# Retention and a gated feed-forward layer on one core: the decay of q moved to y, small loads on another queue, a new written order

## The chip, the cores and the metric

The kernel runs on one core of a Trainium2 chip. The metric is the device time of one execution in microseconds (us); the time before is 329.76 us, the median of 3 runs (329.74 to 330.32). The core has TensorE (matmuls into PSUM), VectorE, ScalarE and GpSimd, each with a list of its own that it works through in order, and SP, whose list here is the queue of loads.

## The reference

```
# q, k, v: (4, 8, 768, 64)      gamma[h] = 1 - 2**(-5-h),  scale = 1/8
for t in range(768):
    state = gamma * state + outer(k[:, :, t], v[:, :, t])     # 64 x 64 per head
    y[:, :, t] = scale * q[:, :, t] @ state
x = y as (4, 768, 512)
h = relu(x @ w_in)                                            # 512 -> 1024
c = conv along the sequence, 3 taps per channel, zeros at both ends
out = (h * sigmoid(c)) @ w_out                                # 1024 -> 512
```

All in float32. Retention is computed in blocks: gamma^(t-s) is split into gamma^t on one side and gamma^-s on the other, so that a block is a masked product of q and k, times v, plus q times the state of the blocks before.

## The kernel before, in words

There are 24 steps of 64 tokens, each for two of the four sequences and all eight heads (12 steps per pair of sequences); the first two steps instead take the first 128 tokens of one sequence each (the "wide" steps). A step loads q, k, k with tokens on the partitions, and v, 256 KB each, into one of four `rw` buffers. `scale_q` (VectorE, L729) multiplies q by the table gamma^t, `scale_v` (VectorE) or `scale_v_act` (ScalarE, four activations) multiplies v by gamma^-t; TensorE makes scores, VectorE masks them out of PSUM (`masked`), and TensorE makes y from them ("half" and "mix", which also hold the scores or the state update of another step). `carry` copies the running state from PSUM for the next step. A table serves two steps: `gq_copy` holds the one for steps 0 and 1 of a pair, `gq_more` lets TensorE make those of steps 2 and 4 in PSUM, where `scale_q` reads them, and `make_gq` makes the others on ScalarE out of the first.

Four steps make a unit of the feed-forward layer, six units in all. In unit 0 (`PLAIN` is 1) x is split into a rounded head (`x_head`, ScalarE) and a remainder (`x_rest`, VectorE) straight from y's PSUM bank, and `mm1` makes plain products in two token parts of 8 blocks each (letters A and B in the order). In units 1 to 5 `y_copy` (ScalarE) takes y from PSUM to a buffer, VectorE makes sums of its quarters (`t_13`, `t_2`, `t_4`), heads and remainders are made of both (`xt_head`, `xt_rest`), and seven block products (`fast`, table `SEVEN`) replace eight; `snap` and `sum` put them together. The few first tokens of a unit's first step that still belong to the unit before are `few_head`, `few_sum`, `few_thead`, `few_rest`. Then come the convolution (`conv_tap`, `conv_side`), the gate, its split, and the output matmuls (`mm2`, letter o), whose results ScalarE copies out (`put`) and GpSimd stores. The weights come as 64-bit words and are cut out by ScalarE and VectorE (`w_top`, `w_bits`, `w_head`, `w_rest`).

What each engine does when is written out by hand: `ORDER` holds one string per engine, a letter per task, and the n-th occurrence of a letter is the n-th task with it. `plan` replays the strings with estimated durations, only to choose the buffers and the places where TensorE gets filler matmuls (`keep_warm`). SP issues loads in the order of "DMA", at most 8 in flight: before a load it waits for the eighth load before it.

PSUM has seven rotating banks (`ps`) and one for the state. A bank of y is given back by the instruction that reads y: `y_copy`, or `x_rest` in unit 0.

Of the kernel before, what the change touches and what calls it, by code (L numbers as in the profile page):

```python
# [27 lines left out]
G = 2  # L28
# [36 lines left out]
    1: (0, ("w", 0, 0), "X"), 5: (3, ("s", 0), "Z"), 6: (4, ("s", 1), "X"), 4: (5, ("w", 1, 1), "W"),  # L65
    7: (6, ("s", 2), "X"), 2: (2, ("w", 0, 1), "Y"), 3: (1, ("s", 3), "Z"),
# [9 lines left out]
V_ON_ACT = [*range(WIDE, 8), *range(14, N_STEPS)]  # L76
# [6 lines left out]
        "rrsfsgqfsaatthqaAAAAAhaAhaABBBhaBBBBABhahaohasoCCCIOICCCIOOICCCOOIooIooCooOoooCoCIooIohaOoOhooahaooooooo"  # L83
        "oooooDDDPJoJDDDJPPJDDDJPPoJahaDDDJPPJhaoPoooohaoohaooooooooEEEKQKEEQEKQKEEEKQQKEEEKhaQKoQQhaoooooohaoooo"
        "ohaooFFFLRLohaFFFLRLFRRFFLRLFFFRRLoLoRhahaooooooGGGMoMoSSGGGMoMoSSoGGGMoMoSSGoGGMSMooSuuuuuuuuuuuuuuuuuu"
# [83 lines left out]
def tt(n):  # L169
    return 67 + n / 0.96, 160 + n / 0.96  # L170
# [1216 lines left out]
```

## Time and profile before

| | us |
|---|---|
| median of 3 runs | 329.76 |
| the profiled execution | 331.79 |
| its span | 330.1 |
| TensorE busy | 322.2 |
| VectorE busy | 290.1 |
| ScalarE busy | 221.9 |

A span reaches from the first to the last instruction; the execution's time holds about 1.7 us more. Matmuls are pipelined and overlap in the records, so TensorE's busy time is not a sum of work. "Idle before" is what an engine waited ahead of an instruction, with what ended the wait. PE is TensorE, PEld its weight loads, DVE VectorE, ACT ScalarE, POOL GpSimd; SPq is SP's queue.

### The profile page before, as it was taken

What the parts mean: (1) busy time and instruction counts of PE and PEld (TensorE: products, weight loads), DVE (VectorE), ACT (ScalarE), POOL (GpSimd) and SP (SyncE); (2) the same over time, 40 slices, a digit from 0 to 9 for tenths busy, and PEclk for the clock granted to TensorE, in tenths of its full rate; (3) what the DMA queues carried; (4) which work ended last, traced back from release to release, by engine and by line L of the source; (5) the groups of instructions that cost most, each with busy time, mean ns of one, the idle gap of its engine ahead of it and who ended that gap; (6) DMA issues with size and microseconds to landing.
All of it is one profiled execution on the core that took longest, in us unless ns stands there. A gap on an engine that the chain in (4) does not pass through costs nothing.

```text
span 330.1 us, 10667 instructions
## 1 busy us (share of the span) xinstructions
PE 322.2 (98%) x4551; PEld 288.2 (87%) x4551; DVE 290.1 (88%) x551; ACT 221.9 (67%) x447; POOL 27.0 (8%) x64
## 2 busy tenths in 40 slices
PE   8999999999999999999999999999999999999995
PEld 5789998988888888999788999888899979998994
DVE  1899999989999999597998368999889999999976
ACT  1589999866668845667758547887557872667440
POOL 2000000001004301100000021000003002000100
PEclk9999999999999999999999999999999999999999
DMA  6996976890006561104743021235002001001103
GB/s 218 401 362 202 312 239 218 305 298 5 3 1 198 189 225 54 43 2 161 223 131 101 0 95 36 89 130 200 3 3 97 2 2 64 0 3 64 66 0 129
DMA packets 21019, 40.21 MB, mean 122 GB/s; under 512 B 2742, under 2 KB 3254, under 8 KB 20972
## 3 DMA queue, kind: packets, MB, share of 16 engines
q1 hardware_dynamic: 19228, 34.15, 30.8%
q0 software_dynamic: 1600, 5.24, 4.2%
q8 instruction: 36, 0.59, 0.7%
q10 hardware_dynamic: 144, 0.13, 0.1%
q14 instruction: 11, 0.09, 0.1%
HBM read 33.23 MB, written 6.29 MB: 120 GB/s over the span
## 4 chain that ended last, share of the span: by engine, by line
PE 73%; DMA 9%; DVE 8%; ACT 7%; SPq 1%; issue 1%; DVEq 0%; ACTq 0%
PE ps L1045 30%; PE ps L1269 30%; PE ps L788 5%; PE ps L1246 5%; PE ps_st L788 3%; DMA rw<-in_qk 3%; DMA w<-in_w_in 2%; DMA w<-in_w_out 2%; DMA rw<-in_kv 2%; SPq L640 1%; DVE hc L1117 1%; DVE t L1260 1%; DVE hc L1077 1%; DVE hc L1127 1%; ACT top L996 1%
## 5 line engine op out<-in xcount | busy, mean ns | idle before, releaser
L1269 PE MATMUL ps<-w,g 128*128 128x512 f32 x480 | 118.3, 397 | 0.5 <-DVE hc L1077 0.5
L1269 PEld LDWEIGHTS ps<-w,g 128*128 128x128 f32 x480 | 87.5, 188 | 19.7 <-DVE hc L1077 0.7
L1045 PE MATMUL ps<-xa,w 128*128 128x256 f32 (+3 forms) x552 | 76.9, 283 | 0.3 <-ACT hc L1089 0.2
L1045 PEld LDWEIGHTS ps<-xa,w 128*128 128x128 f32 x552 | 70.7, 189 | 2.8 <-ACT t L1273 0.5
L1117 DVE SCALAR_TENSOR_TENSOR hc<-hc,cw_sb,hc 128x512 f32<-128x512 f32 (+1 forms) x96 | 68.1, 743 | 1.5 <-ACT hc L1112 1.3
L1045 PE MATMUL ps<-xa,s 128*128 128x256 f32 (+2 forms) x480 | 68.6, 282 | 0.7 <-ACT hc L1072 0.7
L1045 PEld LDWEIGHTS ps<-xa,s 128*128 128x128 f32 x480 | 62.4, 188 | 2.9 <-ACT hc L1072 1.1
L1077 DVE CUSTOM_DVE_ANT_0 hc<-ps,hc 128x256 f32<-128x256 f32 (+2 forms) x80 | 32.2, 418 | 16.0 <-PE ps L1045 11.5
L1072 ACT COPY hc<-ps 128x256 f32<-128x256 f32 (+2 forms) x60 | 22.0, 371 | 31.7 <-PE ps L1045 31.1
L1112 ACT ACTIVATE hc<-hc,cw_sb 128x512 f32<-128x512 f32 x48 | 33.6, 724 | 6.5 <-DVE hc L1077 5.4
L788 PEld LDWEIGHTS ps<-rw 64*64 64x64 f32 (+2 forms) x1472 | 29.1, 137 | 6.0 <-issue 1.4
L788 PE MATMUL ps<-rw 64*64 64x64 f32 (+2 forms) x1472 | 32.7, 225 | 0.7 <-ACT t L882 0.5
L1122 ACT ACTIVATE hc<-hc 128x1024 f32<-128x1024 f32 x24 | 25.3, 1059 | 9.6 <-DVE hc L1117 9.5
L1127 DVE TENSOR_TENSOR hc<-hc,hc 128x1024 f32<-128x1024 f32 x24 | 29.1, 1218 | 1.8 <-ACT hc L1122 1.8
L1135 ACT CAST g<-hc 128x1024 fp32r<-128x1024 f32 x20 | 21.0, 1050 | 13.8 <-DVE hc L1127 13.6
L878 DVE TENSOR_TENSOR xa<-t,xa 128x384 fp32r<-128x384 f32 (+5 forms) x45 | 24.7, 567 | 0.8 <-ACT xa L932 0.3
L1144 DVE TENSOR_TENSOR g<-hc,g 128x1024 fp32r<-128x1024 f32 x20 | 24.4, 1218 | 0.6 <-ACT g L1135 0.4
L788 PE MATMUL ps_st<-rw 64*64 64x64 f32 (+1 forms) x672 | 23.8, 219 | 0.4 <-issue 0.2
L788 PE MATMUL ps<-rw,cy 64*64 64x64 f32 x672 | 23.9, 219 | 0.0
L788 PEld LDWEIGHTS ps_st<-rw 64*64 64x64 f32 (+1 forms) x672 | 21.6, 135 | 2.1 <-issue 0.7
L788 PEld LDWEIGHTS ps<-rw,cy 64*64 64x64 f32 x672 | 21.5, 135 | 0.0
L757 ACT ACTIVATE rw<-rw,const_sb 128x128 f32<-128x128 f32 x64 | 20.2, 394 | 0.0
(89 smaller groups left out, 359.1 us busy)
## 6 DMA issues: line engine op xcount, KB each, us to landing
rw<-in_qk SPq DMA_DIRECT2D x48, 256.0 KB, 4.3
rw<-in_kv SPq DMA_DIRECT2D x46, 256.0 KB, 5.1
out_y<-t POOLq DMA_DIRECT2D x20, 256.0 KB, 2.6
w<-in_w_in SPq DMA_DIRECT2D x16, 256.0 KB, 5.4
w<-in_w_out SPq DMA_DIRECT2D x16, 256.0 KB, 5.6
out_y<-t SPq DMA_DIRECT2D x2, 256.0 KB, 2.4
out_y<-t SPq DMA_DIRECT2D x3, 128.0 KB, 1.7
out_y<-t ACTq DMA_DIRECT2D x1, 128.0 KB, 1.8
```

The costliest lines, as they stand in the source:

```text
L788: nc.tensor.matmul(out, lhsT, rhs, start=start, stop=stop, skip_group_check=True)
L878: nc.vector.tensor_tensor(out=out, in0=in0, in1=in1, op=ALU.subtract)
L1045: nc.tensor.matmul(ps, w(a, k), x(b, k), start=first and i == 0, stop=last, skip_group_check=True)
L1072: nc.scalar.copy(quarter(u, p, *((0, 1), (0, 0), (1, 1))[i]), strip("X", u, p))
L1077: nc.vector._custom_dve(dve_ops.TENSOR_ADD_SAT, out=quarter(u, p, *out), in0=strip(bank, u, p), in1=quarter(u, p, *other), s0=float("inf") ...
L1112: nc.scalar.activation(cv, h, AF.Copy, scale=w)
L1117: nc.vector.scalar_tensor_tensor(out=cv, in0=h, scalar=w, in1=cv, op0=ALU.mult, op1=ALU.add)
L1122: nc.scalar.activation(cv, cv, AF.Sigmoid)
L1127: nc.vector.tensor_tensor(out=cv, in0=h, in1=cv, op=ALU.mult)
L1135: nc.scalar.copy(g_of(u, p)[:, 0], cv_of(u, 2 * p))
L1144: nc.vector.tensor_tensor(out=lo, in0=cv_of(u, 2 * p), in1=hi.bitcast(F32), op=ALU.subtract)
L1269: nc.tensor.matmul(ps, g, w, start=(f == 0 and i == 0), stop=(f == NF - 1 and i == 2))
```

## The change

q is no longer scaled. `y_scale` on VectorE reads y from PSUM, multiplies it by the table and writes the buffer that `y_copy` wrote; `y_copy` is gone, and steps 2 and 3 of unit 0 pass through that buffer too. The tables of steps 2 and 4 are copied out of PSUM by ScalarE (`gq_keep`). v of steps 8 to 11 is scaled by ScalarE. The blocks of y lie in another order in their bank, so that one multiplication with a broadcast table serves both sequences; `SEVEN` and the constants follow, and some copies of unit 0 are cut into more pieces. The loads of the three small tables are issued by ScalarE, and the sigmoid that loads ScalarE's function table is a task in its order. All orders are new.

```diff
 SEVEN = {
-    1: (0, ("w", 0, 0), "X"), 5: (3, ("s", 0), "Z"), 6: (4, ("s", 1), "X"), 4: (5, ("w", 1, 1), "W"),
-    7: (6, ("s", 2), "X"), 2: (2, ("w", 0, 1), "Y"), 3: (1, ("s", 3), "Z"),
+    1: (1, ("w", 0, 0), "X"), 5: (6, ("s", 0), "Z"), 6: (4, ("s", 1), "X"), 4: (5, ("w", 1, 1), "W"),
+    7: (3, ("s", 2), "X"), 2: (2, ("w", 0, 1), "Y"), 3: (0, ("s", 3), "Z"),
...
-V_ON_ACT = [*range(WIDE, 8), *range(14, N_STEPS)]
+V_ON_ACT = [*range(WIDE, NC), *range(14, N_STEPS)]
...
-        "rrsfsgqfsaatthqaAAAAAhaAhaABBBhaBBBBABhahaohasoCCCIOICCCIOOICCCOOIooIooCooOoooCoCIooIohaOoOhooahaooooooo"
...
+        "rrsffgsqsaatthaqAAAAAAhaAhaABBBhaBBBBBhahaohasoCCCIOICCCIOICOoOCCoIoIooOoOooooCCCIooIohaoOOhaoooohaooooo"
...
     "DVE": (
-        "kkmmmqttmmbbllq9mrrbbllbblq9bl0mq9lrBrq800bqmlyyzz9dbmbqqvellrmr3322r4342m4qjr3j2j468jyzm0mIbbCyCzbbOIdC"
...
-        "re332244rqd3jjj2e4m6mj8hLFimhRFFFyLzRyzyLzFyFzRddyyFzzLRerFr332244err33jj2244djjiehGGyyMSizyzyzzGdMGSedy"
...
+        "kkmmmmbbmlttlr9rmbqblbblll9bblrmq9Brlq8m009yyzzq0dmbbellrm3q2r43m2rq34jr23j244qj6j8mmyyzzbI0bCCdOlCCeIyO"
...
+        "2e44d4jjq6ejj8mmhLiFmFqhRFLFyRyzzyLyFzzRdFdeyFyzzRrr332244qqerr3322jj4F4djjLiehGGyMzSiyyyzzzGddSMeGayyzz"
...
     "ACT": (
-        "qkaawwvcxxaawwaAaAwcvwa0w0AxvczxA0y5vaBctwBtBAAaacgkBeywwBvvxxkyxBcAhhyxchtBBy5h7A0ctCaaCCaCwawCgCeCttCw"
...
+        "rblaaqqwwxvnxcaacwaawwwAAvxaazwwAAAvxc0q5c00BvtBtvaBcgAakeAwwBBxvtxcxvhcxhkAh5h7BBBtaCa0CaCwCgCCewttCvwa"
...
     "DMA": (
-        "qrbkqkgqkwvwwwvvqwktwwwwwwwvqwwckvtqkqtqvwwtkwwwwqqvvvkkttktwvqkqwtwwwkwwvvwtwwtwwqqkkvtqktqkvvvttqkvtqq"
-        "vkttkqtvkvqkqqvvvkkqttttvkooooo"
+        "qqqkkkwwwwvvvtqkwwwwwwwwwvwtwwcqkvqktqqvwwvktwwqqkvvttkkvqktqkwwwwwqkwtvvvwwttwwwwqtkqttvvqvktkqtkqkqvkv"
+        "qkttqvktvvtqvtkqkvqttvkooooo"
...
-    load(("load_rows",), 2 * H * len(TERMS) * ROWS, take=[("hc", "rows")])
-    load(("load_c",), 4 * P * N_GVF)
-    load(("load_g",), 4 * P * 54, [("load_rows",)])
+    task(("load_rows",), ACT, (430, 3400), take=[("hc", "rows")])
+    task(("load_g",), ACT, (430, 3000), [("load_rows",)])
+    task(("load_c",), ACT, (430, 3500), [("load_g",)])
+    task(("table",), ACT, (1500, 1500), [("load_c",)])
...
-            decay = ("make_gq", n - c % 2) if c > 1 else ("gq_copy",)
-            if decay[-1] in GQ_ON_PE:
-                decay, at = ("gq_more", n - c % 2), GQ_ON_PE.index(n - c % 2)
-                if c % 2 == 0:
+            decay = ("gq_copy",)
+            if c > 1:
+                m = n - c % 2
+                decay = ("gq_keep" if m in GQ_ON_PE else "make_gq", m)
+                if m == n and m in GQ_ON_PE:
+                    at = GQ_ON_PE.index(n)
                     after = [("gq_more", GQ_ON_PE[at - 1]) if at else ("gq_rows",), ("load_g",)]
-                    pe(decay, 230, after, [("ps", ("gq", n))], [("hc", "rows")] * (n == GQ_ON_PE[-1]), 1)
-            if decay == ("make_gq", n):
-                task(decay, ACT, (1180, 1280), [("gq_copy",), ("load_c",)], [("gq", n)])
-            task(("scale_q", n), DVE, tt(512), [("load_q", n), decay], free=[("ps" if decay[0] == "gq_more" else "gq", ("gq", n - 1) if decay[0] == "gq_more" else n - 1)] if c % 2 and c > 1 else [])
+                    pe(("gq_more", n), 230, after, [("ps", ("gq", n))], [("hc", "rows")] * (n == GQ_ON_PE[-1]), 1)
+                    task(decay, ACT, act(512, 45), [("gq_more", n)], [("gq", n)], [("ps", ("gq", n))])
+                elif m == n:
+                    task(decay, ACT, (1180, 1280), [("gq_copy",), ("load_c",)], [("gq", n)])
...
             if own:
-                pe(("scores", n), 960, [("scale_q", n), ("load_k", n)], banks, count=32)
+                pe(("scores", n), 960, [("load_q", n), ("load_k", n)], banks, count=32)
...
                     after += [scaled, ("masked", n, 0)]
-                    after += [extra and ("scale_q", extra), extra and ("load_k", extra)]
+                    after += [extra and ("load_q", extra), extra and ("load_k", extra)]
...
+        if not wide:
+            table = [("gq", n - 1)] if c % 2 and c > 1 else []
+            task(("y_scale", n), DVE, tt(512), [("mix", n), decay], [("t2", ("y", n))], [y] + table)
         if u < PLAIN:
-            task(("x_head", n), ACT, act(512, 45), [("mix", n)], [("xa", u)] * (n == first))
-            task(("x_rest", n), DVE, tt(512), [("x_head", n)], free=[y])
+            task(("x_head", n), ACT, act(512, 45 + 85 * (not wide)), [("mix" if wide else "y_scale", n)], [("xa", u)] * (n == first))
+            task(("x_rest", n), DVE, tt(512), [("x_head", n)], free=[y if wide else ("t2", ("y", n))])
             continue
-        task(("y_copy", n), ACT, act(512, 45), [("mix", n)], [("t2", ("y", n))], [y])
...
-    table = const.tile([P, 1], F32, name="table")
-    nc.scalar.activation(table, warm[:, :1].bitcast(F32), AF.Sigmoid)
+    table_sb = const.tile([P, 1], F32, name="table")
+
+    @emits
+    def table():
+        nc.scalar.activation(table_sb, warm[:, :1].bitcast(F32), AF.Sigmoid)
...
-    def fetch(out, in_):
-
+    def fetch(out, in_, small=False):
+
+        if small:
+            nc.scalar.dma_start(out, in_)
+            return
...
-        if n - n % 2 in GQ_ON_PE:
-            return buf("ps", ("gq", n - n % 2)).rearrange("p (g t) -> p g t", g=NPAIR)
         return buf("gq", n - n % 2).rearrange("p (g t) -> p g t", g=NPAIR)
+
+    @emits
+    def gq_keep(n):
+        nc.scalar.copy(buf("gq", n), buf("ps", ("gq", n)))
...
-    @emits
-    def scale_q(n):
-        q, s = heads_of(n)[:, 0], n % 2
-        decay = gq_of(n)[:, :, s * C : (s + 1) * C].unsqueeze(1).broadcast_to([P, G, NPAIR, C])
-        nc.vector.tensor_tensor(out=q, in0=q, in1=decay, op=ALU.mult)
...
     def place_of(n, k, b):
-        return (2 * k + b - (UNIT_OF[n] >= PLAIN)) % 4
+        if n < WIDE:
+            return 2 * k + b
+        return 2 * b + 1 - k if UNIT_OF[n] < PLAIN else 2 * b if k else 3 - 2 * b
...
-        y, x, t = y_of(n).rearrange("p (k b) g c -> p k (b g) c", k=2), plain_x(1), n * C - PARTS[1][0]
-        return [(y, [x[:, i].rearrange("p k b g t -> p k (b g) t")[:, :, :, t : t + C] for i in range(2)])]
+        y, x, t = copied(n).rearrange("p (b k) g c -> p b k g c", k=2), plain_x(1), n * C - PARTS[1][0]
+        return [(y[:, :, 1 - k], [x[:, i, k, :, :, t : t + C] for i in range(2)]) for k in range(2)]
...
-    def y_copy(n):
-        nc.scalar.copy(buf("t2", ("y", n)), buf("ps", ("y", n)))
+    def y_scale(n):
+        s = n % 2 * C
+        y, out = (a.rearrange("p (q g c) -> p q g c", q=2, g=NPAIR) for a in (buf("ps", ("y", n)), buf("t2", ("y", n))))
+        decay = gq_of(n)[:, :, s : s + C].unsqueeze(1).broadcast_to([P, 2, NPAIR, C])
+        nc.vector.tensor_tensor(out=out, in0=y, in1=decay, op=ALU.mult)
...
-            nc.scalar.copy(x[:, 0, 1:], y[:, :3])
-            nc.scalar.copy(x[:, 0, 0], y[:, 3])
+            nc.scalar.copy(x[:, 0, 2:], y[:, :3:2])
+            for at, q in ((0, 3), (1, 1)):
+                nc.scalar.copy(x[:, 0, at], y[:, q])
...
-            difference(x[:, 1, 1:], y[:, :3], hi[:, 1:])
-            difference(x[:, 1, 0], y[:, 3], hi[:, 0])
+            difference(x[:, 1, 2:], y[:, :3:2], hi[:, 2:])
+            for at, q in ((0, 3), (1, 1)):
+                difference(x[:, 1, at], y[:, q], hi[:, at])
...
+    order = [2, 3, 0, 1]
     gq = scale * gamma[:, :, None] ** t[:P]
-    one = np.repeat(np.eye(2), D, axis=1).astype(_BF16)
+    one = np.repeat(np.eye(2)[::-1], D, axis=1).astype(_BF16)
     tables = [gq] + [scale * gamma[:, :, None] ** t[n * C : n * C + P] for n in GQ_ON_PE]
-    tables = zip(*(_pieces(x) for x in tables))
+    tables = zip(*(_pieces(x[:, order]) for x in tables))
...
-    gf = gamma[:, None, None, :] ** (P * np.arange(NC * C // P)).reshape(1, 1, -1, 1)
+    gf = gamma[::-1, None, None, order] ** (P * np.arange(NC * C // P)).reshape(1, 1, -1, 1)
...
```

## Rows read from the trace of the kernel before

**Rows 1.** The page, section 1: busy us (share of the span) xinstructions of each engine.
```profile
PE 322.2 (98%) x4551; PEld 288.2 (87%) x4551; DVE 290.1 (88%) x551; ACT 221.9 (67%) x447; POOL 27.0 (8%) x64
```
**Rows 2.** Waits of TensorE: line <- releaser: us in total, times, longest.
```profile
PE ps L1045 <- ACT hc L1072: 0.7, 1, 0.7
PE ps L788 <- ACT t L882: 0.5, 1, 0.5
```
**Rows 3.** Busy us (x instructions) by stretch; then TensorE's clock, DMA share, GB/s.
```profile
10.00:20.00 10.00, 9.85 (x244) 7.69 (x244) 9.46 (x18) 7.77 (x17) 0.00 (x0) 1.00 1.05 397
20.00:30.00 10.00, 10.00 (x195) 9.43 (x188) 9.48 (x17) 9.22 (x18) 0.00 (x0) 1.00 0.85 295
...
50.00:60.00 10.00, 9.31 (x386) 8.24 (x388) 9.96 (x24) 9.36 (x24) 0.50 (x2) 1.00 0.64 205
...
250.00:260.00 10.00, 10.00 (x113) 9.35 (x114) 9.93 (x18) 6.61 (x12) 1.96 (x3) 1.00 0.21 80
```
**Rows 4.** Timeline of TensorE: start us, us, engine line op out<-in xcount [idle before <-releaser].
```profile
21.07 7.35 PE L1045 MATMUL ps<-xa,w 128*128 128x256 f32 x60
...
157.03 1.65 PE L1269 MATMUL ps<-w,g 128*128 128x512 f32 x6
...
160.15 5.80 PE L1269 MATMUL ps<-w,g 128*128 128x512 f32 x24 [0.47 <-DVE hc L1077]
...
263.24 8.62 PE L1269 MATMUL ps<-w,g 128*128 128x512 f32 x36
271.94 0.97 PE L1045 MATMUL ps<-xa,w 128*128 128x254 f32 x6
...
274.90 1.55 PE L1269 MATMUL ps<-w,g 128*128 128x512 f32 x6
...
277.00 1.55 PE L1269 MATMUL ps<-w,g 128*128 128x512 f32 x6
```
**Rows 5.** Timeline of SP, which issues the loads, from the start.
```profile
0.82 0.37 SPq L640 DMA_DIRECT2D rw<-in_qk  x1
1.24 0.42 SPq L640 DMA_DIRECT2D hc<-in_rows  x1
...
2.10 1.30 SPq L640 DMA_DIRECT2D rw<-in_qk  x3
```
**Rows 6.** Stretches of 1 us near the start (columns as in rows 3).
```profile
3.00:4.00 1.00, 1.00 (x29) 0.87 (x28) 0.00 (x0) 0.00 (x0) 0.31 (x2) 1.00 0.82 162
4.00:5.00 1.00, 0.93 (x10) 0.27 (x4) 0.00 (x0) 0.00 (x0) 0.00 (x0) 1.00 0.68 178
5.00:6.00 1.00, 1.00 (x3) 0.50 (x2) 0.98 (x2) 0.00 (x0) 0.00 (x0) 1.00 1.06 399
```
**Rows 7.** Groups by line: names, shapes xcount | busy us, mean ns | idle before.
```profile
L1077 DVE CUSTOM_DVE_ANT_0 hc<-ps,hc 128x256 f32<-128x256 f32 (+2 forms) x80 | 32.2, 418 | 16.0 <-PE ps L1045 11.5 <-ACT hc L1072 3.7
...
L757 ACT ACTIVATE rw<-rw,const_sb 128x128 f32<-128x128 f32 x64 | 20.2, 394 | 0.0
...
L846 DVE TENSOR_TENSOR rw<-ps,mask 128x512 f32<-128x512 f32 x22 | 14.9, 683 | 0.5 <-PE ps L788 0.5
...
L882 ACT COPY t<-ps 128x512 f32<-128x512 f32 x20 | 11.7, 584 | 3.7 <-PE ps L788 3.7
...
L732 DVE TENSOR_TENSOR rw<-rw,gq 128x512 f32<-128x512 f32 x16 | 10.9, 685 | 2.4 <-DMA rw<-in_qk 2.4
...
L626 ACT ACT_TABLE_LOAD x1 | 1.3, 1283 | 0.8 <-PEq L1376 0.8
```
**Rows 8.** Timeline of ScalarE near the start.
```profile
2.10 0.20 ACT L626 ACTIVATE table<-warm 128x1 f32<-128x1 f32 x1
...
12.79 1.39 ACT L996 CAST top<-w 128x512 f16<-128x512 bf16 x2
```
**Rows 9.** Timeline of VectorE near 157 us and near 271 us.
```profile
156.49 0.69 DVE L732 TENSOR_TENSOR rw<-rw,gq 128x512 f32<-128x512 f32 x1 [2.36 <-DMA rw<-in_qk]
...
270.33 1.42 DVE L878 TENSOR_TENSOR xa<-t,xa 128x512 fp32r<-128x512 f32 x2
```

More of the change, by code (lines that the diff above doesn't have):

```diff
@@ L82 @@
     "PE": (
[L83 to L85 removed]
+        "rrsffgsqsaatthaqAAAAAAhaAhaABBBhaBBBBBhahaohasoCCCIOICCCIOICOoOCCoIoIooOoOooooCCCIooIohaoOOhaoooohaooooo"
+        "oooooDDDJPJDDPDJPoJDDDJPPoJahaDDDJPPJhaohaPooooooohaooooooEEEKoKEEEKQQQKEEEKQQKEEEKQQKhaoQhaoohaoooohaoo"
+        "oooooFFFLoRLhaFFFLRLRFRFFLRLFFRFLoLoRRhahaooooooGGGMoMoSSGGGMoMoSSooGGGMoMoGSSGGMoMoSSuuuuuuuuuuuuuuuuuu"
         "uuuuuuuuuuuuuuuuuuuuuuuuuuuuuuuuuuuuuu"
@@ L126 @@
 FETCH, FETCH_NS, BEHIND, PACKET_LAG = (61.0, 126.6, 127.3), (600, 2300), 0, {2: 1300, 6: 300, PE: 1100, ACT: 900}
-FIRST = {PE: 3850.0, DVE: 1200.0, ACT: 3200.0, POOL: 2500.0, DMA: 700.0}
+FIRST = {PE: 3850.0, DVE: 1200.0, ACT: 810.0, POOL: 2500.0, DMA: 700.0}
 WARM_UP, WARM_SMALL, WARM_NS = 4, 14, 232
@@ L150, in ops @@
     if name == "few_head":
-        return 1 + (UNIT_OF[k[1]] == PLAIN)
-    return 2 if name == "few_rest" or (name in ("g_head", "g_rest") and k[1] == LAST[0]) else 1
+        return 1 + 2 * (UNIT_OF[k[1]] == PLAIN)
+    if name in ("x_head", "x_rest") and k[1] in range(WIDE, UNITS[0]):
+        return 2
+    if name == "few_rest":
+        return 2 + (UNIT_OF[k[1]] == PLAIN)
+    return 2 if (name in ("g_head", "g_rest") and k[1] == LAST[0]) else 1
 def halves(n):
@@ L274, in list_tasks @@
         few = TOKENS[u][0] - FIRST_STEP[u] % NC * C if n == first else 0
+        if not wide:
+            table = [("gq", n - 1)] if c % 2 and c > 1 else []
+            task(("y_scale", n), DVE, tt(512), [("mix", n), decay], [("t2", ("y", n))], [y] + table)
         if u < PLAIN:
-            task(("x_head", n), ACT, act(512, 45), [("mix", n)], [("xa", u)] * (n == first))
-            task(("x_rest", n), DVE, tt(512), [("x_head", n)], free=[y])
+            task(("x_head", n), ACT, act(512, 45 + 85 * (not wide)), [("mix" if wide else "y_scale", n)], [("xa", u)] * (n == first))
+            task(("x_rest", n), DVE, tt(512), [("x_head", n)], free=[y if wide else ("t2", ("y", n))])
             continue
-        task(("y_copy", n), ACT, act(512, 45), [("mix", n)], [("t2", ("y", n))], [y])
         if few and u > PLAIN:
-            task(("few_head", n), ACT, act(6 * few), [("y_copy", n)])
-            task(("few_sum", n), DVE, (450, 550), [("y_copy", n)])
+            task(("few_head", n), ACT, act(6 * few), [("y_scale", n)])
+            task(("few_sum", n), DVE, (450, 550), [("y_scale", n)])
             task(("few_thead", n), ACT, act(8 * few), [("few_sum", n), ("few_head", n)])
@@ L285, in list_tasks @@
         elif few:
-            task(("few_head", n), ACT, (170, 280), [("y_copy", n)])
-            task(("few_rest", n), DVE, (160, 260), [("few_head", n)])
+            task(("few_head", n), ACT, (255, 365), [("y_scale", n)])
+            task(("few_rest", n), DVE, (235, 335), [("few_head", n)])
         t = C - few
-        task(("x_head", n), ACT, act(6 * t), [("y_copy", n)], [("xa", u)] * (n == first))
+        task(("x_head", n), ACT, act(6 * t), [("y_scale", n)], [("xa", u)] * (n == first))
         task(("x_rest", n), DVE, tt(6 * t), [("x_head", n)])
@@ L665, in load_c @@
     def load_c():
-        fetch(const_sb, consts)
+        fetch(const_sb, consts, True)
     def row_tile():
@@ L672, in load_rows @@
     def load_rows():
-        fetch(row_tile(), rows)
+        fetch(row_tile(), rows, True)
     def table_of(j):
@@ L697, in load_g @@
     def load_g():
-        fetch(low_tile(), low)
+        fetch(low_tile(), low, True)
     @emits
```

14 lines of the change are left out of this document (7 added, 7 removed), and 6 rows, old and new, of the table LETTER.

## The prediction

> **What bounds the kernel now.** I read the shares of the engines first. TensorE is busy 322.2 of 330.1 us, and VectorE and ScalarE far less [rows 1]. Busy time alone does not prove a bound, so I went on to what TensorE waited for: its longest named waits after the start are 0.7 and 0.5 us [rows 2]. So from its first feed-forward matmul at 21.07 us [rows 4] nearly the whole span is TensorE work laid end to end. The change adds, takes or reshapes no matmul. It can therefore win only in four places: before 21 us, while TensorE is fed late; between 20 and 60 us, where VectorE and ScalarE are nearly full too; at a stall near 157 us; and around 264 us, where VectorE is full again.
>
> The table by stretches shows the second place: in the first and the last of the four stretches from 20 to 60 us VectorE is busy 9.5 and 10.0 of 10 us and ScalarE 9.2 and 9.4, while ScalarE still has 2.2 us free between 10 and 20 us [rows 3]. The start of SP's list shows the first: q, two small tables, then three more q and k loads [rows 5]; from 3 to 5 us the DMA engines move 162 and 178 GB/s, against 399 right after [rows 6].
>
> The profiled execution took 331.79 us, 1.7 more than its span, and 2.03 us more than the median 329.76 of the runs. I sum differences against the profiled execution and take them off the median.
>
> **The change, part by part.** *VectorE's decay.* Twenty-two multiplications of q (0.685 us for those with the table in SBUF) go, and twenty-two of y come. The new ones read PSUM; the nearest row is the mask, which also takes a PSUM operand and a broadcast one: 0.683 us [rows 7]. Count and duration are equal, so the sum is zero. The extra PSUM read could cost 0 to 0.02 us each by these rows. What changes is when: q of step n was scaled about two steps ahead of the matmuls that use y of step n. Deferring it takes some two multiplications, 1.4 us, out of VectorE's work before 62 us, and puts them back near the end.
>
> *v on ScalarE for steps 8 to 11.* Each takes four activations of 0.394 us from ScalarE, 1.6 us, and frees 0.68 us of VectorE. One of the four steps falls before 62 us.
>
> *The copy of y.* Twenty copies of 0.584 us [rows 7] leave ScalarE, five of them before 62 us: 2.9 us. Two copies of a decay table out of PSUM come: 1.2 us. The matmul that refills y's bank now waits for VectorE, 0.683 in place of 0.584 us, so a prompt release is 0.1 us later; at the one place where TensorE waited for that copy (0.5 us) I expect the same wait.
>
> *The plain steps 2 and 3.* y used to be split straight from PSUM; now a multiplication stands ahead, and the head and the remainder are two instructions each. For step 4's few tokens, ScalarE's head becomes three small copies (one column took 0.20 us [rows 8]) and VectorE's remainder three. The first matmul of the second token part waits for exactly this. I price it at +0.4 us of late start (0 if other work lies in between, 0.7 if none does).
>
> *The table load.* The activation-function load (1.28 us) is now ScalarE's first instruction, at 0.8 us [rows 7], where nothing waits. After the change the first sigmoid stands behind the scaling of v of step 2, about 16 us. Either the one load moves there or a second one appears there: +1.3 us of ScalarE in both cases, +0 if the load stays at the head. I take 1.3. Two places behind it in ScalarE's list stands the carry copy that step 2's matmuls need.
>
> The row with the first activation shows it starting at 2.10 us [rows 8], directly after the load's end at 0.81 + 1.28. The Trainium skill, page "ScalarE: Activation LUTs", section "What ACT_TABLE_LOAD costs", puts a switch at about 2.66 us, because a drain follows the load. The trace disagrees for a load with nothing ahead of it; no run here shows one in mid-stream. By the page's figure ScalarE would lose 1.4 us more, and my gain at the start would be gone.
>
> *Small loads from ScalarE's queue.* Three loads leave SP's list, each about 0.4 us of issue [rows 5], and q, k of steps 0 to 2 go out back to back. They land while ScalarE is idle: its first weight step is at 12.79 us [rows 8]. If the stream is full from 3 us on, the 0.8 MB that 399 GB/s would move in those 2 us replaces 0.34 MB, so everything behind is 1.15 us earlier [rows 6]. k of step 0 now stands fourth of the big loads in place of second, which eats that gain for the first scores alone; I expect them at about 6.4 us still.
>
> Walking the new lists on from there, with about 0.6 us from start to start for a 512-column step on VectorE or ScalarE and TensorE's groups at their old lengths: first scores 6.4 to 8.5, two flips, second scores to 11.0, third to 12.3, both wide mixes to 13.4. VectorE: four masks to 12.4, two weight steps, a mask, a remainder, then the two tables of k at 15.3 and 16.0; TensorE's states to 17.0. ScalarE: v of step 2 to 15.8, the table load to 17.3, x's second head to 17.8, the carry to 18.4. Then VectorE's second remainder of x ends at 19.3, TensorE's mix of step 2 at 19.5, a table matmul at 19.8, and the first feed-forward matmul starts at 19.9 us: **-1.2 us** against 21.07. The lower bound is -1.9, if the six blocks now issued in a row all find their weights; the upper is 0.
>
> *What is left at 62 us.* VectorE: -1.4 - 0.7 + 0.5 for the extra small instructions = -1.6 us. ScalarE: -2.9 + 1.2 + 1.6 + 1.3 + 0.3 = +1.5 us, against 2.2 us of free time between 10 and 20 us, which the earlier weights let it use. So ScalarE does not cut the gain to nothing, but it leaves no room. I keep -1.2 + 0.4 = **-0.8 us** (between -1.9 and +1.9).
>
> *The stall near 157 us.* VectorE stood 2.36 us, waiting for q of a later step to land, because scaling q was next in its list [rows 9]. TensorE paid: one block of six 512-column and one of six 254-column matmuls took from 157.03 to 160.15, 3.12 us, where the same pair took 2.10 from 274.90 to 277.00 [rows 4]. After the change no VectorE instruction waits for a q load, and TensorE needs that q some 9 us later. **-1.0 us** (0 if another late input takes its place).
>
> *The last unit.* Before its first matmul TensorE has 36 output matmuls, 8.62 us from 263.24, and starts at 271.94; VectorE's last remainder ends at 270.33 + 1.42 = 271.75 [rows 4, 9]. So the cover is used up to 0.2 us, with VectorE 9.9 of 10 us busy [rows 3]. Now two multiplications of y (1.4 us) come into this stretch, and two short sums (0.418 us each, [rows 7]) move to later places in VectorE's list, one of them only behind part of the chain. Net +0.5 to +1.0 us on a chain with 0.2 of slack, of which I let the shorter work ahead absorb half: **+0.3 us** (0 to +1.2).
>
> Sum: -0.8 - 1.0 + 0.3 = -1.5 us: 330.3 us as profiled, 328.3 us as median.
>
> **Rivals.** *The whole early gain arrives* (-1.9 at the start, the few tokens covered, no loss at the end, 157 us gone): -2.9, 326.9 us. For it: VectorE has 1.6 us less in its fullest stretch. Against it: ScalarE's surplus.
>
> *It does nothing that counts*: the chain before 62 us ends in late transfers in both orders, and the 157 us stall is replaced by another late input. Weights of the second layer load behind q and k in the new list as well, so the 0.7 us wait near 67 us [rows 2] may grow by as much as the start gives. 329.7 us.
>
> *Slower: ScalarE becomes the bound of the first 62 us.* Its place is the stretch from 20 to 60 us, with 0.8 and 0.6 us free in its first and last 10 us [rows 3]. If it can't use its free time before 20 us (weights landing no earlier), its surplus of 1.5 us and the 0.4 us of the few tokens reach TensorE whole: +1.9, less 1.0 at 157 us, plus 0.3 at the end: +1.2, 331.0 us. It decides once ScalarE regains less than about 0.6 us of its idle time. A table load that held ScalarE twice as long as its row's 1.28 us would by itself use that up. (The Trainium skill's figure on the page named above is about that long.)
>
> **Numbers.** Chances: my forecast 0.47 (by itself 327.3 to 329.2), the whole gain 0.16, nothing 0.18, slower 0.19. A measurement of this kernel tells about 0.2% from no change, 0.66 us. Faster holds my forecast nearly whole and the whole gain, 0.62; same is the third case and a little, 0.19; slower 0.19. The range runs from 326.5 to 331.0 and leaves out some 0.2 at its ends.
>
> **What would show it.** Right: the first feed-forward matmul near 20 us; DMA near 400 GB/s from 3 us on; no VectorE wait on a q load at 157 us; ScalarE's total 2.5 to 4 us lower; VectorE's total 2 us lower; TensorE's work equal. A table load of 1.28 us near 16 us with the carry copy behind it shows that step. Wrong: the first such matmul at 21 us or later, TensorE waiting for ScalarE between 30 and 60 us for over 2 us in sum, or a gap of over 1 us ahead of the last unit.

## The result, and the profile of the changed kernel

Predicted were 328.3 us (326.5 to 331.0) and "faster". Measured, on one chip and in ten runs each: 330.37 us before, 332.16 us after, a ratio of 1.0055 [1.0035, 1.0075]. The change costs 1.8 us: slower, not faster, and outside the range.

The page of the changed kernel answers to [rows 1] with its engine line and its chain of waits by engine:

```profile
PE 323.1 (98%) x4551; PEld 289.8 (88%) x4551; DVE 287.3 (87%) x550; ACT 218.5 (66%) x449; POOL 29.9 (9%) x64
...
PE 94%; DVE 2%; DMA 1%; ACT 1%; issue 1%; SPq 0%; DVEq 0%
```

VectorE has 2.8 us less to do and ScalarE 3.4 us less (2 and 2.5 to 4 were predicted), and TensorE has the same 4551 matmuls. The kernel is still TensorE's work laid end to end, and yet longer. So I looked for the loss between matmuls, and compared the two kernels at landmarks that stand behind the same tasks in both TensorE orders. Each column is one profile; before and after were profiled twice.

| us, start of | before | before again | after | after again |
|---|---|---|---|---|
| first scores | 6.41 | 6.41 | 7.44 | 6.78 |
| first feed-forward matmul | 21.07 | 21.13 | 21.14 | 19.79 |
| unit 1 | 62.78 | 62.94 | 63.40 | 62.43 |
| the last unit | 271.94 | 270.23 | 271.66 | 270.10 |
| the output's last stage (the seven blocks) | 306.00 | 304.29 | 306.20 | 304.65 |
| last matmul | 325.71 | 323.99 | 326.03 | 324.49 |
| end of the span | 330.09 | 328.35 | 330.76 | 329.34 |

Against "before again", the mean of the two executions of the changed kernel gains 0.67 us up to 21 us, loses 0.64 from there to unit 1, 0.68 from unit 1 to the last unit, 0.48 in the last unit, 0.14 after it and 0.43 behind the last matmul: 1.70 us, against 1.8 in the medians. Two executions of one kernel lie up to 1.7 us apart in this table, so the split shows where to look; it proves no single term.

TensorE's named waits from 16 us on, first of the changed kernel, then of the kernel before in its second profile (columns: total us, times, longest):

```profile
PE ps L801 <- issue: 1.0, 2, 0.6
PE ps L1063 <- ACT hc L1107: 0.5, 1, 0.5
PE ps L1063 <- ACT hc L1090: 0.3, 1, 0.3
PE ps_st L801 <- ACT cy L867: 0.2, 1, 0.2
```

```profile
PE ps L788 <- ACT t L882: 0.5, 1, 0.5
PE ps L1045 <- ACT hc L1072: 0.3, 1, 0.3
PE ps L1045 <- ACT hc L1089: 0.2, 1, 0.2
PE ps_st L788 <- ACT cy L854: 0.2, 1, 0.2
```

Two things are new: a 0.5 us wait for L1107, ScalarE's activation at unit 1, and 1.0 us of "issue", stops for which the profile names no releaser. One is gone: the 0.5 us for the copy of y (L882). The new multiplication itself cost what it should, by the list of its line (duration min/median/max in ns):

```profile
L898 DVE TENSOR_TENSOR t<-ps,gq x20: 675/682/692, 21.7 to 263.6; 128x512 f32<-128x512 f32 x20
...
L898 DVE TENSOR_TENSOR t<-ps,gq_sb x2: 680/680/680, 148.1 to 151.1; 128x512 f32<-128x512 f32 x2
```

ScalarE's records of the start show the table load twice, as L1014's cast took a load of its own; each lasted 1.28 us, and the next instruction began 20 ns behind each end:

```profile
9.48 1.28 ACT L1014 ACT_TABLE_LOAD   x1 [9.48 <-DMA w<-in_w_in]
10.78 1.40 ACT L1014 CAST top<-w 128x512 f16<-128x512 bf16 x2
...
15.93 1.28 ACT L768 ACTIVATE rw<-rw,const_sb 128x128 f32<-128x128 f32 x4
17.22 1.28 ACT L638 ACT_TABLE_LOAD   x1
18.52 0.20 ACT L638 ACTIVATE table<-warm 128x1 f32<-128x1 f32 x1
18.62 0.57 ACT L948 CAST xa<-ps 128x512 fp32r<-128x512 f32 x1
19.09 0.59 ACT L867 COPY cy<-ps_st 128x512 f32<-128x512 f32 x1
```

The Trainium skill, page "ScalarE: Activation LUTs", section "What ACT_TABLE_LOAD costs", adds a drain of about 1.38 us; neither load here shows one.

### The profile page after: what moved, and what is told of

Its sections match the earlier page's. It is cut to its first block, busy times and chain, and to the rows that moved or that the text cites. A ratio compares the mean times of both kernels' runs of the same rounds, so it can differ in the third digit from the quotient of the medians.

```text
span 330.8 us, 10664 instructions
## 1 busy us (share of the span) xinstructions
PE 323.1 (98%) x4551; PEld 289.8 (88%) x4551; DVE 287.3 (87%) x550; ACT 218.5 (66%) x449; POOL 29.9 (9%) x64
## 4 chain that ended last, share of the span: by engine, by line
PE 94%; DVE 2%; DMA 1%; ACT 1%; issue 1%; SPq 0%; DVEq 0%
PE ps L1063 37%; PE ps L1287 33%; PE ps L801 11%; PE ps L1264 6%; PE ps_st L801 4%; PE ps L645 2%; DMA w<-in_w_out 1%; DVE xa L891 1%; SPq L655 0%; DVE t L891 0%; PE ps L756 0%; ACT rw L768 0%; DVE t L1278 0%; DVE t L898 0%; ACT xa L975 0%
## 5 line engine op out<-in xcount | busy, mean ns | idle before, releaser
L1063 PE MATMUL ps<-xa,w 128*128 128x256 f32 (+3 forms) x552 | 76.7, 283 | 0.5 <-ACT hc L1107 0.5
L1063 PEld LDWEIGHTS ps<-xa,w 128*128 128x128 f32 x552 | 70.9, 189 | 2.9 <-ACT hc L1107 0.9
L1063 PE MATMUL ps<-xa,s 128*128 128x256 f32 (+2 forms) x480 | 68.5, 283 | 0.3 <-ACT hc L1090 0.3
L1063 PEld LDWEIGHTS ps<-xa,s 128*128 128x128 f32 x480 | 62.6, 189 | 2.1 <-ACT hc L1090 0.5
L1090 ACT COPY hc<-ps 128x256 f32<-128x256 f32 (+2 forms) x60 | 22.2, 370 | 38.7 <-PE ps L1063 38.1
L891 DVE TENSOR_TENSOR xa<-t,xa 128x384 fp32r<-128x384 f32 (+7 forms) x50 | 26.3, 546 | 1.8 <-ACT xa L975 1.0
L768 ACT ACTIVATE rw<-rw,const_sb 128x128 f32<-128x128 f32 x80 | 25.5, 394 | 0.0
```

What stands on the lines that cost most here:

```text
L768: nc.scalar.activation(v[:, :, g], v[:, :, g], AF.Copy, scale=gvf_sb[:, n % NC, g : g + 1])
L891: nc.vector.tensor_tensor(out=out, in0=in0, in1=in1, op=ALU.subtract)
L1063: nc.tensor.matmul(ps, w(a, k), x(b, k), start=first and i == 0, stop=last, skip_group_check=True)
L1090: nc.scalar.copy(quarter(u, p, *((0, 1), (0, 0), (1, 1))[i]), strip("X", u, p))
```

## The experiments

**Was the stall at 157 us real?** The kernel before, unchanged:

> The kernel before, unchanged, for a second profile and for the size of no change. My prediction took its stalls from one profile that took 331.79 us, 1.4 us more than the median 330.37 of ten runs. Theory A: the stall of 1.0 us at 157 us is there in every execution, so the second profile shows VectorE waiting over 2 us for a load of q near 156 us again. Theory B: it belongs to that one execution; then the second profile lacks it, and the gain of 1.0 us in my sum was not there to be had. The ratio to the kernel before should be 1.000 within 0.002 under both.

329.79 us, 0.999 [0.996, 1.0019]. The stall of [rows 9] is gone in this execution: VectorE's wait for a q load, and the two blocks that took 3.12 us in [rows 4] now take 2.20 us (156.34 to 158.54):

```profile
DVE rw L732 <- DMA rw<-in_qk: 0.2, 1, 0.2
```

```profile
156.34 1.65 PE L1269 MATMUL ps<-w,g 128*128 128x512 f32 x6
157.83 0.88 PE L1045 MATMUL ps<-xa,s 128*128 128x254 f32 x6
158.54 1.32 PE L1269 MATMUL ps<-w,g 128*128 128x512 f32 x5
```

The two spans differ by 1.7 us, 1.4 of it between 155 and 160 us: 0.9 in these two blocks and most of the rest in a stop of TensorE just ahead of them. The first profile's execution (331.79) was 1.4 us above the ten-run median. Of the six profiles of kernels with the old decay in this document, it is the only one in which VectorE waits over 0.6 us for a q load, so the stall belongs to some executions, not to the kernel. How many have it is not known.

**The start: the table load and the order of the loads.** Three kernels: the first sigmoid put back behind the small loads, k of step 0 put second of the big loads, and both.

```diff
-"rblaaqqwwxvnx..."   ->   +"rblnaaqqwwxvx..."     # ScalarE (n: the sigmoid); it no longer waits for load_c
-"qqqkkkwwww..."      ->   +"qkqkqkwwww..."        # SP
```

> The changed kernel with the first sigmoid put directly behind ScalarE's three small loads. The trace of after shows two loads of an activation table, 1.28 us at 9.48 us and 1.28 us at 17.22 us, where before had one at 0.81 us. Theory A (the tables and what stands behind them set the start): one load is left, near 2.3 us, x's second head and the carry copy come 1.3 to 1.5 us earlier, and the first feed-forward matmul starts near 20.0 us in place of 21.14; 0.6 to 1.1 us less in all than after. Theory B (ScalarE's second load lies beside VectorE work that ends as late): the first feed-forward matmul stays within 0.3 us of 21.1 and the time within 0.3 us of after's. Theory C (the start may gain, but weights that land near 62 to 67 us set what follows): the first such matmul earlier, the waits of TensorE at 62.5 and 67.0 us (0.65 and 0.42 us) longer by the same amount, time unchanged.

> The changed kernel with its six first big loads in the order q0 k0 q1 k1 q2 k2 in place of q0 q1 q2 k0 k1 k2. In after the first scores start at 7.44 us, before at 6.41. Theory A (k of step 0 as the fourth load is what ate the gain at the start): the first scores start near 6.0 us, the second near 9 us in place of 11.2, and the first feed-forward matmul 0.3 to 1.0 us before 21.14. Theory B (the scores are early enough in both; ScalarE and VectorE set 21 us): first scores 1.2 us earlier, first feed-forward matmul within 0.2 us of 21.14, time within 0.3 us of after's.

> The changed kernel with both edits: the first sigmoid behind the three small loads, and the big loads in the order q0 k0 q1 k1 q2 k2. Theory A (the start is what was lost): first feed-forward matmul at 19.5 to 20.0 us and 1.2 to 1.6 us less than after in all. Theory C (later waits take it back): first such matmul as early, but the waits near 62 to 67 us and at 157 us grow, and the time is within 0.4 us of after's.

All are slower than the changed kernel, though each starts earlier than its first profile (21.14 us; its second started at 19.79): 1.0129 [1.0088, 1.0170], 1.012 [1.0074, 1.0167] and 1.0161 [1.0118, 1.0204], with the first feed-forward matmul at 20.64, 19.95 and 19.05 us but unit 1 only at 65.90, 66.81 and 64.35. One load is left in the first of them:

```profile
2.24 1.28 ACT L638 ACT_TABLE_LOAD   x1 [2.24 <-issue]
3.54 0.20 ACT L638 ACTIVATE table<-warm 128x1 f32<-128x1 f32 x1
```

So what is won at the start is more than given back. TensorE's waits from 16 us on say where, first with the sigmoid moved, then with k of step 0 second:

```profile
PE ps L801 <- issue: 3.4, 2, 2.3
PE ps L1063 <- ACT hc L1107: 0.5, 1, 0.5
PE ps L1287 <- DVE t L898: 0.4, 1, 0.4
```

```profile
PE ps_st L801 <- issue: 4.5, 3, 3.5
```

The table by stretches of the kernel with the sigmoid moved, cut at its two stops (us, then busy us and instructions of TensorE, its weight loads, VectorE, ScalarE and GpSimd, the granted clock, DMA share, GB/s):

```profile
54.50:55.95 1.45, 0.39 (x27) 0.25 (x19) 1.45 (x5) 1.45 (x6) 0.00 (x0) 1.00 0.52 168
55.95:59.50 3.55, 3.55 (x127) 2.93 (x126) 3.01 (x9) 2.91 (x8) 0.00 (x0) 1.00 0.83 286
59.50:62.00 2.50, 0.22 (x15) 0.08 (x7) 1.24 (x5) 1.17 (x3) 0.00 (x0) 1.00 0.93 302
```

Between the stops lie 127 matmuls and 126 weight loads, about 253 instructions. The page's third part lists an instruction queue of 36 packets with 0.59 MB, 16 KB each and one per 126 of the 4551 matmuls, and the DMA view of 59.5 to 62 us shows one of its packets in that stop:

```profile
q8 instruction: 36, 0.59, 0.7%
```

```profile
q8 instruction: 1, 0.02, 2.5%
```

That reads as TensorE standing at the end of a block of its own instructions until the next block is there. The Trainium skill, page "Runtime: NRT & Kernel Launch", section "Instruction fetch mechanics", tells of 16 KiB blocks of 256 instructions and calls the crossing mostly hidden; the trace agrees on the block and shows up to 3.5 us not hidden. A long stop can have a second price, by the stretches of the kernel with k second: the granted clock, 1.00 (2.4 GHz) up to the stop of 3.5 us, falls to 0.57 behind it, so for much of these 4 us it was at the lower level, 1.2 GHz. In the kernel with both edits it stayed at 1.00 behind a stop of 2.5 us.

```profile
58.00:62.00 4.00, 0.64 (x41) 0.50 (x30) 1.58 (x6) 1.50 (x5) 0.00 (x0) 1.00 0.97 321
62.00:66.00 4.00, 3.87 (x73) 3.62 (x74) 2.49 (x9) 1.49 (x6) 0.21 (x1) 0.57 0.41 126
```

**Is it the burst of weight loads ahead of it?** The changed kernel again, and the loads of `w_out` spread out in it and in the kernel with both edits:

```diff
-"...vqktqkwwwwwqkwtvvv..."
+"...vwwqktqkwqkwwwtvvv..."
```

> The changed kernel, unchanged, for a second profile beside the second one of the kernel before (span 328.4 us, against 330.1 in the first). Theory A: what after loses against that second profile, 2.0 us up to the last matmul, is in fixed places: 0.8 us between 60 and 68 us (waits for w_out weights), 0.6 us of waiting for nothing named inside the run of narrow matmuls at 156.5 us, 0.4 us in the last unit. Then the second profile shows the same three within 0.3 us each and a ratio of 1.004 to 1.008. Theory B: these are as accidental as the stall at 157 us was before; then at least two of the three are gone or elsewhere.

> The changed kernel with the loads of w_out between 58 and 63 us spread out: two of five go ahead of q of step 10, one stays, two go behind q and k of step 12. Theory A (weights that land late cost after the waits of 0.3, 0.65 and 0.42 us at 60.9, 62.5 and 67.0 us): these become shorter, 0.3 to 0.9 us less than after. Theory B (those waits are for ScalarE, which is late by itself): they stay, time within 0.3 us of after.

> The kernel with the early start (first sigmoid behind the small loads, q0 k0 q1 k1 q2 k2: first feed-forward matmul at 19.05 us in place of 21.14) and the same spreading of the w_out loads. Without the spreading TensorE stood 2.7 us in the middle of a run of narrow matmuls at 57.8 us, with nothing named as its releaser, while the DMA engines moved 332 to 381 GB/s for five w_out loads issued at about 57 us. Theory A (TensorE there waits for its own next instructions, whose transfer is queued behind that burst): the stall falls under 1.2 us, and the time by 1.5 us or more against 335.1. Theory B (the stall is the cost of fetching instructions inside narrow matmuls, whatever the other transfers do): it stays over 2 us and the time within 0.5 us of 335.1.

332.04 us, 1.0054 [1.0026, 1.0082] again. Of the three places that this profile was to confirm, the wait for L1107 (0.5 us) and the last unit (34.55 us) came again; the wait for L1090 and the stop at 157 us did not. With the loads spread, 1.0067 [1.0041, 1.0094] and 1.0128 [1.0077, 1.0179], and the longest stops stayed at 0.7 and 2.5 us. So spreading these five loads does not help. Other transfers still ran ahead of the 2.5 us stop, at 195 to 348 GB/s from 55 to 59 us, so transfers as such are not ruled out as the cause.

**The small loads alone, in the kernel before:**

```diff
-    load(("load_rows",), ...)      # SP "qrbkqkgqk...", ACT "qkaaww..."
+    task(("load_rows",), ACT, ...) # SP "qkqkqk...",    ACT "rblnqkaaww..."
```

> The kernel before with one part of the change alone: the three small loads issued by ScalarE ahead of its first sigmoid, SP starting with q0 k0 q1 k1 q2 k2. Theory A (this part is good at the start and lost later): first scores near 5.2 us in place of 6.41, first feed-forward matmul 0.5 to 1.2 us before 21.1, and TensorE's waits between 53 and 68 us longer by about as much, time within 0.5 us of before or slower. Theory B (this part alone gains; the loss is in the new order): 0.5 to 1.2 us faster than before.

0.9983 [0.9954, 1.0013], no difference clear of noise: first scores at 5.14 in place of 6.41, but the first feed-forward matmul at 20.95 against 21.13 and unit 1 at 62.88 against 62.94. Most of the gain is gone before 21 us, which neither theory had.

**The waits that carry names.** A sixth buffer for the scaled y; ScalarE's unit-1 activations ahead of two later tasks; both:

```diff
-BUFS = {... 't2': 5 ...}          +BUFS = {... 't2': 6 ...}
-"...xhkAh5h7BBB..."               +"...xhkABh5h7BB..."       # ScalarE
```

> The changed kernel with six in place of five buffers in the pool that takes both the scaled y and the finished output rows. In four of seven profiles of the changed kernel and its variants one multiplication of y stood 0.4 to 1.5 us on VectorE until an output row's transfer out of its buffer had landed (in the second profile of after 1.40 us near 108 us, and TensorE's output matmul behind it 0.66 us); in three profiles of before and its variant the copy of y by ScalarE never did. Theory A (the move of y's bank from ScalarE to VectorE exposes TensorE to that wait): no such wait in the profile, and 0.2 to 0.8 us less than after. Theory B (the wait only fills time that is lost elsewhere): no such wait, time within 0.2 us of after.

> The changed kernel with one of three relu copies that stand behind the few tokens of step 8 in ScalarE's list put two places ahead of them, where ScalarE idles 0.52 us. In all profiles of the changed kernel that start its second unit near 62 us TensorE waits there 0.65 us, put down to this relu by the waits; in before it does not wait there. Theory A (relu, ready since 51 us, holds the PSUM bank because ScalarE's list waits for VectorE's multiplication of y): the first matmul of unit 1 comes 0.2 to 0.65 us earlier, and the time falls by as much. Theory B (the few tokens themselves end as late): the gap stays within 0.2 us, time within 0.2 us of after.

> Both edits of the changed kernel, six buffers and the relu ahead. Theory A: 0.5 to 1.2 us less than after, so within 1.3 us of before. Theory B (neither counts; the loss is in where TensorE stops for its instructions): within 0.3 us of after.

1.0095 [1.0061, 1.0129], 1.0085 [1.0058, 1.0111], 1.006 [1.0037, 1.0083]. The first tested nothing: the planner takes the lowest free number and never hands out the sixth buffer. Its plan is that of the changed kernel, and the third edit's plan is that of the second. So 1.0095 is a third series of the changed kernel, beside 1.0055 and 1.0054, and shows how far one kernel's ratio can move between series. The relu put ahead halves the wait for L1107, but unit 1 starts at 63.35 us against 63.40, as TensorE's stop near 55 us is 0.2 us longer in that execution and another of 0.1 us comes near 60 us. Against the first kernel of the same series the relu's two are 0.4 and 1.1 us faster by the medians, within the intervals. TensorE's two waits at L1063 then:

```profile
PE ps L1063 <- ACT hc L1107: 0.2, 1, 0.2
...
PE ps L1063 <- ACT hc L1090: 0.2, 1, 0.2
```

The buffer was tested with another rule of choice: the one longest free.

```diff
-  i = min(some, key=lambda i: (max(some[i], t), i))
+  i = min(some, key=lambda i: (max(some[i], t), some[i] * (name == "t2"), i))
```

> The changed kernel with another choice among its five buffers that take scaled y and output rows: the one that has been free longest, in place of the free one with the lowest number. With six buffers the planner had never handed out the sixth, so that kernel ran as after and tested nothing; here the multiplication of y of step 10, near 109 us, gets a buffer whose output row left some 5 us earlier. Theory A (TensorE's stop of 0.2 to 0.9 us near 110 us, in five of eight profiles, comes from that buffer): VectorE's wait ahead of this multiplication and TensorE's stop are gone, and the time falls by 0.2 to 0.8 us against after's 332.1. Theory B (the multiplication waits for ScalarE's table of decays or its carry): the wait stays.

332.06 against 330.46 in that series, 1.0035 [1.0011, 1.006]. In the changed kernel's second profile VectorE's step at 109 us waits until its buffer has been written out, and TensorE waits for VectorE:

```profile
109.22 0.69 DVE L898 TENSOR_TENSOR t<-ps,gq 128x512 f32<-128x512 f32 x1 [1.40 <-DMA out_y<-t]
```

```profile
109.97 3.06 PE L1287 MATMUL ps<-w,g 128*128 128x512 f32 x12 [0.66 <-DVE t L898]
```

With the new rule both waits are gone:

```profile
109.08 0.68 DVE L898 TENSOR_TENSOR t<-ps,gq 128x512 f32<-128x512 f32 x1
```

```profile
107.58 5.62 PE L1287 MATMUL ps<-w,g 128*128 128x512 f32 x23
```

The wait is shown and removed; the time won by it, 0.7 us by the ratios, is within their intervals.

**Do the stops move with the instruction count?** Idle matmuls at the start shift every later instruction by a known number: 32 more in the kernel before, 28 fewer in the kernel with both edits, and 8 more in the changed one.

```diff
-WARM_UP, WARM_SMALL, WARM_NS = 4, 14, 232
+WARM_UP, WARM_SMALL, WARM_NS = 4, 30, 232     # 0 and 18 in the others
```

> The kernel before with 30 in place of 14 pairs of small idle matmuls at the start: 32 more matmuls, 0.45 us in the trace's spacing, at a place where TensorE waits 0.36 us for a load; nothing else is changed. All profiles so far show TensorE's longest waits for nothing named at the same matmuls of the program, the 1108th and the 1235th, 127 apart, inside runs of 64-column matmuls. Theory A (TensorE stops where a block of about 127 matmuls' instructions ends if the next is not there yet, so the alignment of these blocks to the narrow runs sets part of the time): the waits move by 32 matmuls to earlier ones of the program, their sum changes, and the time changes by over 1 us, in either direction. Theory B (the waits belong to these places of the program, for instance to late inputs): they stay at the same work, and the time is within 0.5 us of before.

> The kernel with the early start (first feed-forward matmul at 19.05 us, 335.1 us in all) without the 14 pairs of small idle matmuls at the start, so that its instruction blocks end 28 matmuls later in the program. The two stops of 1.1 and 2.7 us at 53 and 58 us stood at its 1108th and 1234th matmul, both inside runs of narrow ones; 28 later the second lies nearer to the end of its run. Theory A (block ends): the stops move by 28 matmuls and their sum of 3.8 us changes by over 1 us, the time with it. Theory B (late inputs of those steps): the sum stays at 3.3 to 4.3 us and the time within 0.6 us of 335.1.

> The changed kernel with 18 in place of 14 pairs of small idle matmuls at the start, 8 matmuls more (0.1 us). Theory A (the loss of after is largely a matter of where its instruction blocks end): the waits for nothing named move by 8 matmuls, and the time changes by more than 0.6 us, up or down; if it falls by 1.5 us or more, the change itself costs nothing. Theory B (the loss is in its waits for VectorE and ScalarE): within 0.4 us of after.

With 32 more the kernel before is at 1.0162 [1.0121, 1.0203], some 5.3 us slower, for matmuls that last 0.5 us in all and stand where TensorE waits for data anyway. Its profile (the fastest of its runs, 333.42) has stops in places where none was, a feed-forward block at 22 us among them:

```profile
PE ps L1045 <- issue: 1.6, 2, 1.0
PE ps_st L788 <- issue: 0.9, 1, 0.9
PE ps L1269 <- issue: 0.5, 1, 0.5
```

Its five longest stops without a releaser stand ahead of the 347th, 853rd, 1107th, 1997th and 2379th matmul of the trace: 4, 2, 7 and 3 times 126 to 128 apart. With 28 fewer, 1.0247 [1.0197, 1.0297], some 2.8 us above its own base by the ratios:

```profile
PE ps L801 <- issue: 4.0, 4, 2.1
```

There the stops between 53 and 64 us stand ahead of the 982nd, 1109th and 1235th matmul, again 127 and 126 apart. Its base stopped ahead of the 1109th and 1235th too, and these are other instructions of the program, 28 matmuls further on. So the stops belong to the count, not to the work. The loss of this kernel is not all in them: its first feed-forward matmul starts at 20.94 us against 19.05. With 8 more the changed kernel gave 331.54, 1.0023 [1.0001, 1.0046]. To see whether the 8 matmuls alone do that:

> The changed kernel with both edits that came out below it: the buffer that has been free longest (ratio to before 1.0035) and 8 more small idle matmuls at the start (1.0023), against 1.0055 of the change alone. Theory A (two separate costs, TensorE's stop at 110 us and a start at half rate): the gains of 0.2 and 0.3% add, ratio 0.998 to 1.002. Theory B (one or both were chance within the intervals of 0.25% each): ratio 1.003 to 1.005.

> The kernel before with the same 8 more small idle matmuls at the start. In the profile of the changed kernel with them TensorE ran at its full rate from 4.4 us on and the first feed-forward matmul started at 19.95 us; in five of seven profiles of the unlengthened changed kernel it ran at half rate until 9 to 10 us and started at 20.8 to 21.4. Theory A (busier TensorE at the start helps any kernel): full rate from about 4.4 us, the first feed-forward matmul before 20.6 us in place of 21.1, and 0.3 to 1 us faster than before. Theory B (block ends, moved by 8): no earlier start; the time changes by the waits for nothing named, in either direction.

> The candidate for a version that beats both: the kernel before, with the small loads issued by ScalarE (ratio 0.9983, interval 0.9954 to 1.0013) and the 8 more small idle matmuls. Theory A (both help the start and nothing behind takes it back): ratio 0.994 to 0.998. Theory B (an earlier start comes to the narrow matmuls near 53 us too early and waits there): ratio 0.999 to 1.004, with TensorE waiting over 1.5 us for nothing named between 52 and 60 us.

The new buffer rule with the 8 matmuls: 1.0032 [1.0008, 1.0056], no better than either. The kernel before with them: 0.9988 [0.9964, 1.0012], nothing, and no earlier start (21.95 us). The kernel before with ScalarE's small loads and the 8 matmuls: 329.12 us, **0.9959 [0.9935, 0.9983]**, faster than the kernel before in the one series that ran it, and by the ratios than the changed one. It keeps its early start, 19.18 us and unit 1 at 61.50, and its stops are few (TensorE's waits from 16 us on):

```profile
PE ps L795 <- ACT t L889: 0.5, 1, 0.5
PE ps_st L795 <- issue: 0.3, 1, 0.3
```

## Why the prediction was wrong

**"The stall near 157 us. -1.0 us."** This step failed outright. The stall stood in the profiled execution, 331.79 us, and not in the second one, 330.06 us; I took its removal off a median of 329.76, which is below both. The prediction notes those 2.03 us and still sums across them. Against an execution without the stall the step was worth 0.

**"What is left at 62 us: -0.8 us."** Measured: 0.0 (62.92 in the mean, against 62.94). Its parts:
- The table load: 1.3 us in mid-stream, right. The second load was among the cases; no theory had that the kernel without it is slower.
- "Everything behind is 1.15 us earlier": half of it. From 3 to 5 us 268 and 331 GB/s came, not 399, by the stretches of the changed kernel:

```profile
3.00:4.00 1.00, 1.00 (x29) 0.87 (x28) 0.00 (x0) 0.00 (x0) 0.32 (x2) 1.00 1.07 268
4.00:5.00 1.00, 1.00 (x10) 0.45 (x5) 0.00 (x0) 0.00 (x0) 0.00 (x0) 1.00 1.03 331
```

  That is 0.26 MB more than before in those 2 us, 0.65 us at 399 GB/s. The first scores came at 7.44 and 6.78, not at 6.4. In the second profile they waited for k, so k of step 0 as fourth load cost more than the stream gave; with k second they came at 5.14. In the first they stood behind idle matmuls that TensorE worked through without a wait, at the slow pace of the next point.
- "The first feed-forward matmul starts at 19.9 us": 21.14 in the first profile, 19.79 in the second. The difference is TensorE's own pace: the same 16 score matmuls and the flips behind them, first and second profile:

```profile
7.44 2.08 PE L801 MATMUL ps<-rw 64*128 64x128 f32 x16
9.46 1.49 PE L756 MATMUL ps<-g,rw 128*128 128x128 f32 x8
```

```profile
6.78 1.16 PE L801 MATMUL ps<-rw 64*128 64x128 f32 x16 [0.61 <-DMA rw<-in_qk]
7.87 1.09 PE L756 MATMUL ps<-g,rw 128*128 128x128 f32 x8
```

  The granted clock reads 1.00 over 6 to 9 us in both. I summed "TensorE's groups at their old lengths", and those were the slow ones. So 19.79 us, close to my 19.9, was reached in part by luck.
- From 21 us on the changed kernel loses what an early start gives, to stops that the profile calls "issue" (0.6 and 0.8 us near 55 us) and to the wait for L1107. The wait of 0.5 us for the copy of y, which I expected to stay, is gone. I looked for a new bound in ScalarE's busy time. What ScalarE added was a place in a list: its unit-1 activations stand behind few-token copies that now wait for VectorE's multiplication. I priced those few tokens at +0.4; TensorE did not wait for them but for what stood behind them, 0.5 us.

**"The last unit: +0.3 us."** The sign and size held, by luck: 34.54 us against 34.06, +0.48. But the block ahead did not slip, as the chain I priced would have it; the delay stands in small gaps inside the unit, as here, where the last block starts 0.89 us behind the one before it and 0.71 is usual:

```profile
263.19 8.63 PE L1287 MATMUL ps<-w,g 128*128 128x512 f32 x36
271.66 0.87 PE L1063 MATMUL ps<-xa,w 128*128 128x254 f32 x6
272.55 0.95 PE L1063 MATMUL ps<-xa,s 128*128 128x254 f32 x6
```

**What was in no term.** 0.68 us between unit 1 and the last unit: the wait for an output buffer near 110 us (0.66 in one of the two profiles), a stop of 0.4 at 157 us, the rest unnamed. And 0.43 us behind the last matmul: the last write lands later. All six profiles of kernels with the old decay have 4.4 us there, those of the changed kernel's family 4.4 or 4.7 to 5.0; why stays open.

**The rivals.** "Slower" gave 331.0 and was nearest in size, but its mechanism, ScalarE as the bound of the first 62 us, is not what happened. "Nothing" described the early gain rightly. I gave both 0.37 together, and too much to a sum whose largest term came from one execution.

**What stays open.** That the stops sit at block ends of TensorE's instructions is shown by their spacing, by the packet in the stop, and by their moving with the count. The traces tell one thing more. Between the two stops of the kernel with the sigmoid moved TensorE needs 3.55 us for its block, and in all 20 profiles of this case it passes these two block ends 2.2 to 3.0 us after the packet of the next block starts. Leave out the kernel with 28 fewer matmuls, whose blocks end elsewhere: where the second end costs under 0.5 us, its packet starts 1.0 to 1.9 us after the first end; where it costs 1.2 to 3.5 us, 2.6 to 4.9 us after. So there is hardly any slack, and a long stop is a packet that starts late. Why it starts late is open. An early start alone does not do it: the last kernel starts at 19.18 us and its packet comes after 1.0 us, while three executions of the changed kernel's plan have 1.3, 1.6 and 2.6. Nor is it shown what sets TensorE's pace in the first 10 us; 8 idle matmuls went with the fast pace in two kernels and not in two others, and the changed kernel's second profile had it without them, so the last kernel's gain is measured but its cause is only likely.

## What to carry to other kernels

Before taking a stall off the time, look whether it is in the executions that make up the median: profile the kernel before twice. In a kernel that is one engine end to end, a stop without a releaser that recurs at equal instruction counts is a cost of its own, and any added or removed instruction ahead of it moves it. A multiplication moved for nothing in its own duration still changes who waits in which list, and when its output buffer must be free.

## What the hardware showed unexpectedly

- TensorE stops of 0.4 to 3.5 us between 50 and 64 us, 126 or 127 matmuls apart, at ends of its instruction blocks; 32 idle matmuls more, 0.5 us of work, cost 5.3 us.
- The same 16 matmuls took 2.08 or 1.16 us in two executions of one kernel, with the granted clock at 1.00 in both.
- A cast as ScalarE's first work brought a table load of its own (1.28 us), and the sigmoid behind it made a second; with the sigmoid first there was one.
